# Weight scaling into PSUM, a PReLU that reads its product from PSUM, and a reordered first phase in a pooled-attention and feed-forward kernel

## The chip, the cores and the metric

The kernel runs on one core of a Trainium2 chip, so one set of engines works: TensorE (PE in the profile, with its weight loads PEld), VectorE (DVE), ScalarE (ACT), GpSimd (POOL) and SyncE (SP), which issues the DMAs. Each engine works through its own instruction list in order; semaphores make it wait for others. SBUF holds operands, PSUM takes matmul results and can be read and written by DVE and ACT. The metric is the device time of one execution in microseconds (us), and the median of several executions stands for a kernel. Beside these times there is one profiled execution with a trace of every instruction.

## The reference

Eight batches of eight heads, 576 positions and head size 64. Keys and values are first averaged over groups of 8 positions, so each query sees 72 keys. The attention output of all 4608 tokens, 512 wide, then goes through a two-layer network of inner size 2048 with a PReLU between.

```python
k_p = k.reshape(B, H, S // 8, 8, D).mean(axis=3)
v_p = v.reshape(B, H, S // 8, 8, D).mean(axis=3)
attn = softmax(q @ k_p.transpose(0, 1, 3, 2) / sqrt(D))
x = (attn @ v_p).transpose(0, 2, 1, 3).reshape(B * S, H * D)
h = x @ w_in
g = maximum(h, 0) + alpha * minimum(h, 0)
return g @ w_out
```

## The kernel before, in words

**Chunks.** The 4608 tokens are worked in nine chunks of 512. For a chunk the kernel makes scores, softmax and the mix with the pooled values (these give four transposed tiles x of 128x512), then the first layer in 16 steps f of 128 inner columns, then the second layer, which sums over the same 16 steps. Every matrix product is made of three fp16 products, because each operand is kept as a pair of fp16 numbers, high and low: low x high, high x low, high x high. A step of the first layer is 12 matmuls of 512 columns into one PSUM bank of the pool ps_h, which has two buffers ("h"). A step of the second layer is 12 matmuls too.

**PReLU.** For each step f, `ffn1_scaled` (ACT, L775) copies the bank h into an SBUF tile t times the per-row scale rp; that is the last reader of the bank, so the bank is free for step f+2 when it ends. `ffn1_prelu` (DVE, L779) then makes max(t x al, t) within SBUF. `ffn1_parts` makes the fp16 pair g: the high part on ACT (L786), the low part on POOL (L789).

**Weights.** The weights arrive as float64, read as pairs of 32-bit words. `load_w` brings two steps' weights in one DMA of 1024 KB into a "big" buffer (12 of them, shared with other inputs); `max_w` (DVE, L238) finds row maxima, from which power-of-two scales are made. `convert` makes fp16 pairs of them, eight tiles for each layer: ACT shifts the low word in place (L641); the high word, scaled, goes into an SBUF tile v (three buffers), by ACT in two halves for the first layer (L651) or by POOL in one piece for three of the eight tiles (L645, `v_pool=3`), by ACT in one piece for the second layer (L655); DVE then puts the words together with two bit operations over 128x1024 elements, L665 (shift v by 3, or the low word) and L669 (or the sign), both in SBUF. Then the fp16 high part is made by ACT (L688, L693) and the low part by POOL (L707 for the first layer; L702 for three of the 16 halves of the second, after one more ACT scaling, L700) or by DVE (L696, the other 13 halves).

**Order.** All of chunk 0, the conversion of the weights, and the attention of chunk 1 stand in one first phase, `start`. There a planner, the class `_Plan`, sets the order on all five engines: every operation has an assumed duration, a rank and the buffers it takes and gives, and at each point the planner emits the operation that could start first, by rank among those that could start almost at once. The ranks come from the table of numbers `RK`. Names of the buffers in the planner: "S" are the two buffers of the PSUM pool ps_s, which scores, pooled keys, maxima and the mix share; "h" the two banks; "v" the conversion tiles. Where PE would be idle for long, the planner puts in idle matmuls (L837). From chunk 1 on the order is not the planner's: a scheduler of the language sets it from the dependencies and its own durations, and the next chunk's attention is woven into the steps of the first layer. There the second layer of chunk c follows, and so on to chunk 8.

**Attention in the first phase.** A softmax of 128 tokens runs: row maxima on DVE (L507), subtraction (L521, for tiles that DVE serves), exp on ACT, sums (L526), L528 and L530 for the reciprocal, the product with it on POOL (L532), copies to fp16 pairs on ACT and POOL (L537, L540, L543), and a DMA that transposes. With four such tiles and the pooled values (L483) the mix (PE, L605) gives x, split into fp16 by ACT (L562) and DVE (L566), both reading PSUM.

Of the kernel before, what the change touches and what calls it, by code (L numbers as in the profile page):

```python
# [9 lines left out]
F32 = mybir.dt.float32  # L10
I32 = mybir.dt.int32
# [44 lines left out]
def _new_b(c):  # L56
# [16 lines left out]
class _Plan:  # L73
# [6 lines left out]

    HOP, DMA_HOP = 0.12, 2.0
# [3 lines left out]
    def __init__(self, fill, **room):  # L85
        self.fill = fill
        self.ops, self.room = [], {k: n * [0.0] for k, n in room.items()}

    def add(self, engine, us, emit, *after, rank=0.0, take=None, give=None):
        op = dict(engine=engine, us=us, emit=emit, after=after, rank=rank, n=len(self.ops),  # L90
                  take=take, give=(give,) if isinstance(give, str) else give or (), end=None)
        self.ops.append(op)
        return op

    def start(self, op, free):
# [3 lines left out]
        if op["take"]:  # L99
            t.append(min(self.room[op["take"]]))  # L100
        return max(t)

    def emit(self):
        free, left = {}, list(self.ops)
        while left:
# [14 lines left out]
            free[op["engine"]] = t + op["us"]  # L120
            op["end"] = t + op["us"] + (self.DMA_HOP if op["engine"] == "SP" else self.HOP)
# [9 lines left out]
def pooled_attention_prelu_ffn(ctx: ExitStack, tc: tile.TileContext, qT, kT, vT, kN, vN, w1, w2, alpha, out):  # L131
# [44 lines left out]
    eight = const.tile([P, 2], I32, name="eight")  # L176
    nc.vector.memset(eight, 8)
# [6 lines left out]
    m1 = const.tile([P, NF], F32, name="m1")  # L184
# [115 lines left out]
    def attention(add, c, bs, rank, begin=False, early=False, k_pool=0, q_cuts=1, on_act=(), on_dve=(), behind=()):  # L300
# [116 lines left out]
        for i, b in enumerate(bs):  # L417
            for j in range(2):
# [10 lines left out]
                kd.append(add("DVE", 0.6, lo, h, *kd[2 * i:], rank=rank, give="f" if j else None))  # L429
        qd = {}  # L430
        for i, (t, ld) in enumerate(ql):
# [4 lines left out]
            for a in range(0, HC, w):  # L436
# [8 lines left out]
                    h, *([qd[1]] if end else []), rank=rk,  # L445
# [8 lines left out]
        for b in bs:  # L454
# [21 lines left out]
            def vfloor(b=b, vr=vr):  # L476
# [8 lines left out]
                op0=ALU.mult, op1=ALU.subtract), x, rank=rank + rks["v"] + 1, give="f")  # L485
# [9 lines left out]
        for i in range(TPC):  # L495
# [24 lines left out]
            else:  # L520
# [12 lines left out]
                out=ex(), in0=ex(), in1=sm().broadcast_to([P, 2, 4, SP]), op=ALU.mult), x, rank=rk)  # L533
# [430 lines left out]
```

## Time and profile before

| | |
|---|---|
| time, median of 3 runs | 891.62 us (888.89 to 892.07) |
| the profiled execution's own time | 890.46 us |
| its span in the trace | 888.8 us |
| granted TensorE clock, mean of the span | 0.983 of full speed |
| PE busy | 847.1 us, 95% of the span |
| DVE, ACT, POOL busy | 452.9, 428.2, 400.5 us |
| mix of chunk 0 starts on PE | 63.2 us |
| first layer of chunk 0 done and second layer started | 118.5 us |
| first layer of chunk 1 starts | 177.3 us |

Times in the trace count from the span's start. A row of the trace's timeline gives start, duration, engine, line, operation, tiles and shapes (out <- in), and in brackets how long the engine had been idle before and what it then waited for. Rows that group instructions give the count, the total busy time, the mean in ns, and the idle time before them by what ended it. In the table of windows each engine's busy time stands for each stretch, with PEclk for the granted clock, 1.00 being full speed. The chain of waits is followed back from the last instruction, at each step to what released it.

### The profile page before, as it was taken

The page shows a single profiled execution, that of the slowest core. Times are in us where ns is not written, and L with a number is a line of the kernel's source. Part 1 is how long each engine was busy: PE and PEld are TensorE (multiplying, and loading weights), DVE is VectorE, ACT ScalarE, POOL GpSimd, SP SyncE. Part 2 cuts the span into 40 slices and gives each one's busy share as a digit, 9 for nine tenths or more (in the row PEclk, how much of TensorE's full clock was granted, in tenths as well). Part 3 has the DMA queues.
Part 4 walks back from the last instruction along what each step waited for, and adds up shares of the span by engine and source line. Part 5 has one row for each costly group of instructions (what it writes and reads, how often), then busy time and mean ns, then how long its engine had stood idle before and what let it go on. Part 6 is the DMA issues. An engine that isn't in the chain of part 4 may idle for free.

```text
span 888.8 us, 11503 instructions
## 1 busy us (share of the span) xinstructions
PE 847.1 (95%) x4447; PEld 411.1 (46%) x4447; DVE 452.9 (51%) x655; ACT 428.2 (48%) x724; POOL 400.5 (45%) x377
## 2 busy tenths in 40 slices
PE   6769997898999999999999999999999999999998
PEld 5444453344444544454445444544454444444443
DVE  4999999758415841583158315831583146112210
ACT  5967785555433643364336433643463346213330
POOL 1387948457714461456144614561456027202320
PEclk9879999999999999999999999999999999999999
DMA  9576312360621171117111611171115003100000
GB/s 339 198 158 268 124 51 51 75 202 9 157 96 40 25 182 56 39 28 192 43 39 28 178 57 38 29 198 37 39 28 119 36 13 70 26 36 12 1 25 24
DMA packets 93639, 74.75 MB, mean 84 GB/s; under 512 B 77040, under 2 KB 77616, under 8 KB 93584
## 3 DMA queue, kind: packets, MB, share of 16 engines
q1 hardware_dynamic: 93584, 74.01, 29.4%
q8 instruction: 35, 0.57, 0.3%
q14 instruction: 20, 0.16, 0.1%
HBM read 45.10 MB, written 9.44 MB: 61 GB/s over the span
## 4 chain that ended last, share of the span: by engine, by line
PE 81%; DVE 11%; POOL 3%; ACT 2%; DMA 2%; issue 2%; SPq 0%; POOLq 0%; ACTq 0%; DVEq 0%
PE o L815 13%; PE o L816 13%; PE o L817 13%; PE h L769 12%; PE h L770 12%; PE h L771 12%; PE x L605 2%; DVE v L665 2%; DVE t L779 2%; DVE m L238 1%; DMA vraw<-vT_dram 1%; PE s L595 1%; PE s L594 1%; PE s L596 1%; PE pl L283 1%
## 5 line engine op out<-in xcount | busy, mean ns | idle before, releaser
L789 POOL TENSOR_TENSOR g<-t,g 128x512 f16<-128x512 f32 x144 | 179.6, 1250 | 337.0 <-ACT g L786 337.0
L779 DVE SCALAR_TENSOR_TENSOR t<-t,al 128x512 f32<-128x512 f32 x144 | 140.5, 980 | 272.9 <-ACT t L775 266.1
L770 PE MATMUL h<-x,w 128*128 128x512 f16 x576 | 219.2, 381 | 2.4 <-DVE x L566 2.4
L769 PE MATMUL h<-x,w 128*128 128x512 f16 x576 | 219.1, 380 | 1.4 <-ACT o L805 1.4
L771 PE MATMUL h<-x,w 128*128 128x512 f16 x576 | 218.8, 380 | 0.0
L816 PE MATMUL o<-w,g 128*128 128x512 f16 x544 | 207.1, 381 | 4.4 <-POOL w L702 2.8
L815 PE MATMUL o<-w,g 128*128 128x512 f16 x544 | 206.7, 381 | 3.3 <-POOL g L789 2.8
L817 PE MATMUL o<-w,g 128*128 128x512 f16 x544 | 204.2, 381 | 0.0
L786 ACT CAST g<-t 128x512 f16<-128x512 f32 x144 | 88.4, 615 | 100.9 <-DVE t L779 100.5
L775 ACT ACTIVATE t<-h,rp 128x512 f32<-128x512 f32 x144 | 97.9, 681 | 67.1 <-PE h L771 63.7
L805 ACT ACTIVATE o<-o,os 128x512 f32<-128x512 f32 x34 | 23.2, 687 | 174.1 <-PE o L817 174.1
L815 PEld LDWEIGHTS <-g 128*128 128x128 f16 x576 | 56.5, 98 | 75.4 <-issue 6.0
L817 PEld LDWEIGHTS <-g 128*128 128x128 f16 x576 | 56.6, 98 | 73.8 <-issue 6.9
L771 PEld LDWEIGHTS <-w 128*128 128x128 f16 x576 | 56.5, 98 | 70.3 <-issue 3.5
L769 PEld LDWEIGHTS <-w 128*128 128x128 f16 x576 | 56.5, 98 | 68.1 <-issue 3.7
L816 PEld LDWEIGHTS <-g 128*128 128x128 f16 x576 | 56.5, 98 | 67.4 <-issue 2.1
L770 PEld LDWEIGHTS <-w 128*128 128x128 f16 x576 | 56.5, 98 | 65.4 <-issue 2.5
L463 POOL TENSOR_TENSOR vraw<-vraw 72x512 f32<-72x512 f32 (+1 forms) x56 | 58.9, 1069 | 56.7 <-DMA vraw<-vT_dram 45.8
L566 DVE SCALAR_TENSOR_TENSOR x<-x,xsc,x 128x512 f16<-128x512 f32 x36 | 25.8, 747 | 69.7 <-ACT x L562 69.7
L532 POOL TENSOR_TENSOR e<-e,sm 128x576 f32<-128x576 f32 x35 | 46.9, 1341 | 25.5 <-DVE sm L530 17.2
L537 ACT CAST apad<-e 128x576 f16<-128x576 f32 x72 | 44.8, 669 | 25.8 <-POOL e L532 18.0
L540 POOL TENSOR_TENSOR apad<-e,apad 128x448 f16<-128x448 f32 x36 | 41.7, 1158 | 3.3 <-ACT apad L537 3.1
(135 smaller groups left out, 886.0 us busy)
## 6 DMA issues: line engine op xcount, KB each, us to landing
w<-w_dram SPq DMA_DIRECT2D x16, 1024.0 KB
out_dram<-o SPq DMA_DIRECT2D x36, 256.0 KB
qraw<-qT_dram SPq DMA_DIRECT2D x17, 512.0 KB
vraw<-vT_dram SPq DMA_DIRECT2D x28, 288.0 KB
kraw<-kT_dram SPq DMA_DIRECT2D x12, 576.0 KB
kq<-kT_dram SPq DMA_DIRECT2D x2, 576.0 KB
nat<-kN_dram SPq DMA_DIRECT2D x2, 512.0 KB
nat<-vN_dram SPq DMA_DIRECT2D x2, 512.0 KB
```

The lines of the kernel that those rows point to most:

```text
L463: nc.gpsimd.tensor_tensor(out=o, in0=y, in1=z, op=ALU.add)
L532: x = add("DVE" if i in on_dve else "Pool", us, lambda ex=ex, sm=sm, eng=eng: eng.tensor_tensor(out=ex(), in0=ex(), in1=sm().broadcast_to( ...
L769: nc.tensor.matmul(ps, w[:, 1, ks_], x[:, 0], start=(n == 0), stop=False)
L770: nc.tensor.matmul(ps, w[:, 0, ks_], x[:, 1], start=False, stop=False)
L771: nc.tensor.matmul(ps, w[:, 0, ks_], x[:, 0], start=False, stop=(n == NK - 1))
L775: nc.scalar.activation(t, hps.pop((c, f)), AF.Copy, scale=rp[:, f:f + 1])
L779: nc.vector.scalar_tensor_tensor(out=t, in0=t, scalar=al[:, f:f + 1], in1=t, op0=ALU.mult, op1=ALU.max)
L786: nc.scalar.copy(out=g[:, 0], in_=t)
L789: nc.gpsimd.tensor_tensor(out=g[:, 1], in0=t, in1=g[:, 0], op=ALU.subtract)
L815: nc.tensor.matmul(ps, g[:, 1, ts_], w[:, 0], start=(f == 0), stop=False)
L816: nc.tensor.matmul(ps, g[:, 0, ts_], w[:, 1], start=False, stop=False)
L817: nc.tensor.matmul(ps, g[:, 0, ts_], w[:, 0], start=False, stop=(f == NF - 1))
```

## The change

Six edits:

1. In 14 of the 16 weight tiles (`ps1=6` of the first layer's eight, `ps2=8` of the second's) the first scaling of the high word is written to PSUM, to a buffer of the pool ps_s ("S"), in place of SBUF. Both bit operations of DVE then have one operand in PSUM (L660, L663, formerly L665, L669); the second writes its result to the SBUF tile v, and only then is the S buffer given back.
2. `ffn1_prelu` (now L776) takes its first operand from the bank h in PSUM and multiplies by ra = rp x al instead of al; t is the second operand as before. So DVE's PReLU, not ACT's scaling, is the last reader of the bank, in all nine chunks. ra costs one small POOL product for each of four groups (L725).
3. No tile's first scaling is on POOL any more: the three POOL operations (L645) become six halves on ACT (L653). The unused variant with the shift on POOL is gone, with its constant `eight`.
4. All 16 low halves of the second layer's weights are made on DVE (`w2_dve=16`): three POOL products (L702) and three ACT scalings (L700) become three DVE operations (L691, formerly L696).
5. The small product `ds` (L585, formerly L581) is a tensor_scalar in place of a scalar_tensor_tensor.
6. The planner has a rule for a shared port: POOL operations, and DVE operations marked `two=`, are not planned to overlap. Bit operations with a PSUM operand and the PReLU are not marked. Durations and all ranks in `RK` are new, which gives a new order for the first phase.

```diff
-RK = dict(k_pool=1, sh1_pool=0, sh2_pool=0, v_pool=3, s_pool=0, w2_dve=13, lo_dve=0, l1=392.23, step=2.57,
+RK = dict(k_pool=1, ps1=6, ps2=8, s_pool=0, w2_dve=16, lo_dve=0, l1=405.5, step=2.27, l2=548.61, mx1=198.3,
...
+        if op["two"]:
+            t.append(self.port)
         return max(t)
...
+            if op["two"]:
+                self.port = t + op["us"]
...
-    m1 = const.tile([P, NF], F32, name="m1")
+    m1 = ra = const.tile([P, NF], F32, name="m1")
...
-                nc.vector.scalar_tensor_tensor(out=ds[a:z], in0=eq[c, i // 2][a:z], scalar=2.0 ** -32,
-                                               in1=ek[b][a:z], op0=ALU.mult, op1=ALU.mult)
+                nc.vector.tensor_scalar(out=ds[a:z], in0=eq[c, i // 2][a:z], scalar1=2.0 ** -32,
+                                        scalar2=ek[b][a:z], op0=ALU.mult, op1=ALU.mult)
...
+        ps = once(lambda: ps_s.tile([P, 2, CH], F32, tag="s", name="vw"))
+        by_ps = wide and picked(i, RK[f"ps{l}"], NF // 2)
+        u, kind = (ps, "S") if by_ps else (v, "v")
...
-        if l == 1 and picked(i, RK["v_pool"], NF // 2):
-            x = add("Pool", 2.4, lambda: nc.gpsimd.tensor_tensor(
-                out=v(), in0=word(l, i, 1), in1=y1[:, 2 * i:2 * i + 2].broadcast_to([P, 2, 512]), op=ALU.mult),
-                begin, rank=rank, take="v")
-        elif l == 1:
+        if l == 1:
             x = begin
             for j in range(2):
-                x = add("ACT", 0.61, lambda j=j: nc.scalar.activation(
-                    v()[:, j], word(l, i, 1)[:, j], AF.Copy, scale=y1[:, 2 * i + j:2 * i + j + 1]),
-                    begin, x, rank=rank, take=None if j else "v")
+                x = add("ACT", 0.66, lambda j=j: nc.scalar.activation(
+                    u()[:, j], word(l, i, 1)[:, j], AF.Copy, scale=y1[:, 2 * i + j:2 * i + j + 1]),
+                    begin, x, rank=rank, take=None if j else kind)
...
         if wide:
-            x = add("DVE", 1.5, lambda: nc.vector.scalar_tensor_tensor(
-                out=vi(), in0=word(l, i, 1).bitcast(I32), scalar=-2 ** 31, in1=vi(),
-                op0=ALU.bitwise_and, op1=ALU.bitwise_or), x, rank=rank, give="big" if i % 2 else None)
+            x = add("DVE", 1.22, lambda: nc.vector.scalar_tensor_tensor(
+                out=u().bitcast(I32), in0=u().bitcast(I32), scalar=3, in1=word(l, i, 0).bitcast(I32),
+                op0=ALU.logical_shift_left, op1=ALU.bitwise_or), x, low, rank=rank, two=not by_ps)
+            x = add("DVE", 1.22, lambda: nc.vector.scalar_tensor_tensor(
+                out=v().bitcast(I32), in0=word(l, i, 1).bitcast(I32), scalar=-2 ** 31, in1=u().bitcast(I32),
+                op0=ALU.bitwise_and, op1=ALU.bitwise_or), x, rank=rank, two=not by_ps,
+                take="v" if by_ps else None, give=(*(["big"] if i % 2 else []), *(["S"] if by_ps else [])))
...
-        nc.scalar.activation(t, hps.pop((c, f)), AF.Copy, scale=rp[:, f:f + 1])
+        nc.scalar.activation(t, hps[c, f], AF.Copy, scale=rp[:, f:f + 1])
...
-        nc.vector.scalar_tensor_tensor(out=t, in0=t, scalar=al[:, f:f + 1], in1=t, op0=ALU.mult, op1=ALU.max)
+        nc.vector.scalar_tensor_tensor(out=t, in0=hps.pop((c, f)), scalar=ra[:, f:f + 1], in1=t,
+                                       op0=ALU.mult, op1=ALU.max)
```

The first place where the order differs and that matters below is on DVE in the softmax of the fourth token tile of chunk 0, from the subtraction of the maxima to the reciprocal. "pt" and "pr" belong to reductions of maxima over partitions, "e_123" (after: "e_121"), "rp" and "y" to scales of the first layer's weights, "ev" and "vs__" to the scale of the pooled values. Before:

```order
L521 TENSOR_TENSOR e<-s,mx 128x576
L208 TENSOR_REDUCE pt<-pm 128x1
L213 TENSOR_SCALAR pr<-pt 128x1
L226 TENSOR_SCALAR e_123<-pr 128x4
L229 TENSOR_SCALAR ev_528<-pr 128x1
L718 TENSOR_SCALAR rp<-e_123 128x4
L234 TENSOR_SCALAR vs__532<-ev_528 128x1
L526 TENSOR_REDUCE sm<-e 128x8
L718 TENSOR_SCALAR y_127<-rp 128x4
L528 TENSOR_SCALAR sm<-sm 128x8
L718 TENSOR_SCALAR rp<-rp 128x4
L530 RECIPROCAL sm<-sm 128x8
```

The same place with the change:

```order
L525 TENSOR_TENSOR e<-s,mx 128x576
L242 TENSOR_REDUCE vm<-vs 72x1
L530 TENSOR_REDUCE sm<-e 128x8
L212 TENSOR_REDUCE pt<-pm 128x1
L217 TENSOR_SCALAR pr<-pt 128x1
L532 TENSOR_SCALAR sm<-sm 128x8
L233 TENSOR_SCALAR ev_518<-pr 128x1
L534 RECIPROCAL sm<-sm 128x8
```

The three small operations on the weights' scale (L718, now L713) have moved behind the reciprocal, and the sum of the softmax stands closer to its subtraction.

The second place is on DVE from the last split of x to the second step of the first layer of chunk 0. "x" is the attention's output, "m_125" (after: "m_123") are maxima of the second layer's weights, "w_" loaded weights, "vw" a weight tile in PSUM. Before:

```order
L665 SCALAR_TENSOR_TENSOR v<-v,w_272 128x1024
L566 SCALAR_TENSOR_TENSOR x_676<-x,xsc,x_676 128x512
...
L566 SCALAR_TENSOR_TENSOR x_688<-x,xsc,x_688 128x512
L238 TENSOR_REDUCE m_125<-w_664 128x2
L669 SCALAR_TENSOR_TENSOR v<-w_272,v 128x1024
L779 SCALAR_TENSOR_TENSOR t<-t,al 128x512
L238 TENSOR_REDUCE m_125<-w_686 128x2
L238 TENSOR_REDUCE m_125<-w_707 128x2
L779 SCALAR_TENSOR_TENSOR t<-t,al 128x512 x2
```

With the change:

```order
L663 SCALAR_TENSOR_TENSOR v<-w_217,vw 128x1024
L570 SCALAR_TENSOR_TENSOR x_663<-x,xsc,x_663 128x512
L570 SCALAR_TENSOR_TENSOR x_666<-x,xsc,x_666 128x512
L242 TENSOR_REDUCE m_123<-w_605 128x2
L570 SCALAR_TENSOR_TENSOR x_687<-x,xsc,x_687 128x512
L570 SCALAR_TENSOR_TENSOR x_693<-x,xsc,x_693 128x512
L713 TENSOR_SCALAR rp<-rp 128x6
L660 SCALAR_TENSOR_TENSOR v<-v,w_241 128x1024
L660 SCALAR_TENSOR_TENSOR vw<-vw,w_270 128x1024
L776 SCALAR_TENSOR_TENSOR t<-h,m_122,t 128x512
L663 SCALAR_TENSOR_TENSOR v<-w_241,v 128x1024
L663 SCALAR_TENSOR_TENSOR v<-w_270,vw 128x1024
```

Ahead of the first split of x stand 11 bit operations of the first layer's weights before, and eight with the change; the other eight now stand among the PReLUs.

The third place is on PE where the first layer of chunk 0 ends and the second begins: "g" are the outputs of the PReLU, "s" scores of chunk 1, "idle" matmuls without use. Before, 38 idle matmuls stand there (a weight load and a matmul each) and the 60 score matmuls of chunk 1 come later, behind the seventh step of the second layer and after:

```order
L771 MATMUL h<-x_688,w_282 128x512
L837 LDWEIGHTS pool
L837 MATMUL idle<-pool 128x256
...
L815 LDWEIGHTS g
L815 MATMUL o<-w_664,g 128x512
```

With the change 36 score matmuls of chunk 1 stand there:

```order
L768 MATMUL h<-x_693,w_280 128x512
L598 LDWEIGHTS q_982
L598 MATMUL s<-kbd_95,q_982 128x144
...
L600 MATMUL s<-kbd_95,q_982 64x144
L813 LDWEIGHTS g
L813 MATMUL o<-w_605,g 128x512
```

The remaining 24 of the 60 score matmuls come after the third and the fourth step of the second layer.

More of the change, by code (lines that the diff above doesn't have):

```diff
@@ L86, in __init__, with add @@
         self.fill = fill
-        self.ops, self.room = [], {k: n * [0.0] for k, n in room.items()}
-    def add(self, engine, us, emit, *after, rank=0.0, take=None, give=None):
+        self.ops, self.room, self.port = [], {k: n * [0.0] for k, n in room.items()}, 0.0
+    def add(self, engine, us, emit, *after, rank=0.0, take=None, give=None, two=False):
         op = dict(engine=engine, us=us, emit=emit, after=after, rank=rank, n=len(self.ops),
-                  take=take, give=(give,) if isinstance(give, str) else give or (), end=None)
+                  take=take, give=(give,) if isinstance(give, str) else give or (), end=None,
+                  two=two or engine == "Pool")
         self.ops.append(op)
@@ L428, in attention @@
                 h = add("ACT", 0.53, hi, scs[0], rank=rank)
-                kd.append(add("DVE", 0.6, lo, h, *kd[2 * i:], rank=rank, give="f" if j else None))
+                kd.append(add("DVE", 0.6, lo, h, *kd[2 * i:], rank=rank, give="f" if j else None, two=True))
         qd = {}
@@ L444, in attention @@
                     op0=ALU.mult, op1=ALU.subtract),
-                    h, *([qd[1]] if end else []), rank=rk,
+                    h, *([qd[1]] if end else []), rank=rk, two=True,
                         give="big" if end else "aT" if early and a + w == HC else None)
@@ L638, in convert @@
         v = once(lambda: wp.tile([P, 2, 512], F32, tag="v", name="v", bufs=ROOM["v"]))
-        by_pool = wide and picked(i, RK[f"sh{l}_pool"], NF // 2)
-        if wide and not by_pool:
-            low = add("ACT", 1.2, lambda: nc.scalar.activation(
+        ps = once(lambda: ps_s.tile([P, 2, CH], F32, tag="s", name="vw"))
+        by_ps = wide and picked(i, RK[f"ps{l}"], NF // 2)
+        u, kind = (ps, "S") if by_ps else (v, "v")
+        if wide:
+            low = add("ACT", 1.15, lambda: nc.scalar.activation(
@@ L706, in convert @@
         dve = l == 1 and picked(i, RK["lo_dve"], NF // 2)
-        x = add("DVE" if dve else "Pool", 1.5 if dve else 2.4, lambda: (nc.vector if dve else nc.gpsimd).tensor_tensor(
-            out=part(1), in0=v(), in1=part(0), op=ALU.subtract), x, rank=rank + RK[f"lo{l}"], give="v")
+        x = add("DVE" if dve else "Pool", 1.25 if dve else 2.3, lambda: (nc.vector if dve else nc.gpsimd).tensor_tensor(
+            out=part(1), in0=v(), in1=part(0), op=ALU.subtract), x, rank=rank + RK[f"lo{l}"], give="v", two=dve)
         return [x, x]
@@ L718, in small @@
             return add("DVE", 0.2, lambda: nc.vector.tensor_scalar(
-                out=out, in0=in0, scalar1=s1, scalar2=s2_, op0=op0, op1=op1), x, rank=rank)
+                out=out, in0=in0, scalar1=s1, scalar2=s2_, op0=op0, op1=op1), x, rank=rank, two=True)
         x = add("DVE", 0.2, lambda: floor2(r[0], e1[:, fs], wide), x, rank=rank)
```

43 lines of the change are left out of this document (16 added, 27 removed).

## The prediction, made before the changed kernel ran

> **What bounds the kernel now.** I read the table of windows first, cut where one stage of the kernel hands over to the next: attention of chunk 0 (to 67), first layer of chunk 0 (to 118.5), second layer of chunk 0 (to 170.7), then the chunks after it.
>
> ```profile
> core 0: us, PE busy (x) PEld busy (x) DVE busy (x) ACT busy (x) POOL busy (x), PEclk, DMA share, GB/s
> 0.00:67.06 67.06, 44.68 (x251) 30.49 (x252) 52.73 (x99) 48.14 (x102) 32.35 (x35) 0.87 0.74 233
> 67.06:118.52 51.46, 47.38 (x231) 22.85 (x231) 49.36 (x51) 39.37 (x56) 42.34 (x25) 0.97 0.42 167
> 118.52:170.67 52.15, 45.41 (x244) 21.60 (x244) 49.10 (x61) 34.40 (x74) 34.19 (x32) 0.93 0.33 75
> ...
> 260.00:800.00 540.00, 540.00 (x2867) 257.84 (x2866) 244.07 (x360) 235.91 (x380) 226.97 (x226) 1.00 0.25 65
> ```
>
> From 260 to 800 PE is busy for 540.00 of 540.00 us at full clock: nothing can be gained there, only lost. In the second and third rows DVE is busy for 49 of 51 to 52 us, which is the bound of the first phase (PE's 47.38 there holds idle matmuls too). The chain of waits says the same where the first layer of chunk 0 ends:
>
> ```profile
> 102.63 1.22 DVE m L238
> ...
> 112.79 1.99 DVE v L665
> 114.78 0.16 DVE s L752
> ...
> 114.96 0.73 ACT w L693
> ...
> 116.51 1.97 POOL w L702
> 118.52 0.38 PE o L816
> ...
> 119.33 0.22 PE o L816
> ```
>
> The second layer's first matmul hangs on DVE's row of maxima and bit operations, then on ACT and POOL. In the last row PE goes on at 0.216 us a matmul (0.22 in the chain), so that a step of 12 matmuls takes 2.59 us when nothing stops it.
>
> Third, what DVE does in the first 171 us, in groups by form (busy us and mean ns of one stand behind the bar):
>
> ```profile
> L665 DVE SCALAR_TENSOR_TENSOR v<-v,w 128x1024 int32<-128x1024 int32 x16 | 25.4, 1589 | 0.0
> L669 DVE SCALAR_TENSOR_TENSOR v<-w,v 128x1024 int32<-128x1024 int32 x16 | 21.8, 1364 | 0.0
> L779 DVE SCALAR_TENSOR_TENSOR t<-t,al 128x512 f32<-128x512 f32 x16 | 17.7, 1129 | 0.4 <-ACT t L775 0.4
> L696 DVE SCALAR_TENSOR_TENSOR w<-v,s,w 128x512 f16<-128x512 f32 x13 | 15.1, 1174 | 0.9 <-ACT w L693 0.8
> L581 DVE SCALAR_TENSOR_TENSOR ds<-e 128x1 f32<-128x1 f32 x4 | 4.6, 1151 | 0.0
> L645 POOL TENSOR_TENSOR v<-w,y 128x1024 f32<-128x1024 f32 x3 | 7.0, 2329 | 11.1 <-DVE y L718 9.7 <-issue 1.4
> L702 POOL TENSOR_TENSOR w<-v,w 128x512 f16<-128x512 f32 x3 | 4.4, 1460 | 6.7 <-ACT v L700 6.7
> L651 ACT ACTIVATE v<-w,y 128x512 f32<-128x512 f32 x10 | 7.1, 752 | 0.0
> ```
>
> These means are longer than the same operations need alone, as the timeline shows:
>
> ```profile
> 48.47 2.12 POOL L707 TENSOR_TENSOR w<-v,w 128x1024 f16<-128x1024 f32 x1
> 48.50 0.15 DVE L229 TENSOR_SCALAR ev<-pr 128x1 int32<-128x1 int32 x1
> 48.58 2.04 DVE L718 TENSOR_SCALAR rp<-e 128x4 int32<-128x4 int32 x1
> ...
> 57.52 1.22 DVE L665 SCALAR_TENSOR_TENSOR v<-v,w 128x1024 int32<-128x1024 int32 x1
> ...
> 114.85 0.74 DVE L779 SCALAR_TENSOR_TENSOR t<-t,al 128x512 f32<-128x512 f32 x1
> ```
>
> L718 works on four elements a row and takes 2.04 us, until POOL's L707 is done at 50.59; the 128x1 operation beside it takes 0.15. So some DVE operations with SBUF operands wait out a running POOL operation. Against 1.22 and 0.74 us alone, the groups lose 16 x 0.37 = 5.9 us (L665), 16 x 0.14 = 2.3 (L669), 16 x 0.39 = 6.2 (L779), 13 x 0.43 = 5.6 (L696, of L779's shape) and 4 x 1.0 = 4.0 (L581, against 0.15): 24 us together. An operation of the same kind with a PSUM operand, in the whole run:
>
> ```profile
> L566 DVE SCALAR_TENSOR_TENSOR x<-x,xsc,x 128x512 f16<-128x512 f32 x36 | 25.8, 747 | 69.7 <-ACT x L562 69.7
> ```
>
> Its mean over 36 is 0.747, the time alone: it never waited. The change makes 28 of the 32 bit operations and all PReLUs of this kind.
>
> **The change, stage by stage.** *To the mix of chunk 0.* The softmax of the fourth token tile is last before the mix:
>
> ```profile
> 45.80 0.74 DVE L507 TENSOR_REDUCE mx<-s 128x8 f32<-128x576 f32 x1
> ...
> 52.02 0.20 DVE L530 RECIPROCAL sm<-sm 128x8 f32<-128x8 f32 x1
> ...
> 63.23 1.93 PE L605 MATMUL x<-aT,v 88*64 88x512 f16 x16 [1.37 <-DVE v L665]
> ...
> 67.86 0.58 PE L770 MATMUL h<-x,w 128*128 128x512 f16 x1 [2.38 <-DVE x L566]
> ```
>
> From maxima to reciprocal are 6.4 us. With the three L718 and their 128x4 maxima behind it, there remain maxima, subtraction, another reduction and the sum at 0.74 each and five small ones at 0.15: 3.7, so -2.7 us. Ahead of the split of x, DVE has eight bit operations for 11: 3 x 1.22 = -3.7, of which 2.38 is the wait of L770 on L566. Together -6.4 us. Against it, ACT gets the six halves for L645: 6 x 0.752 = 4.5 us; ACT was busy for 48.14 of 67.06, so idle time covers most, and I charge 0.9. This stage: -5.5; bounds -2 (only the wait of L770 goes) and -8 (the port waits of L645 go as well, 3 x 0.5).
>
> *First layer of chunk 0.* DVE now has 16 PReLUs (11.8 us at 0.74), 16 bit operations (19.5 at 1.22), 8 maxima (9.8 by L238's 1.22), 4 splits (3.0) and 4 of L691 (3.0), which is 47.1; key sums and products and small ones I put at 6, an estimate from rows between 0.15 and 1.4 us; 48 of these start 0.07 before the one ahead ends, -3.4. That is 49.7, plus 1 to 2 us of port waits on what remains in SBUF: 51 against 51.46, so -0.5, bounds -4 and +3. DVE stays the bound here and is still what frees the h banks, now by the PReLU, behind which bit operations stand: a late PReLU delays the matmuls of step f+2. But the stage now does more: 16 bit operations of the 32 where nine or ten were, and at its end 36 scores in place of idle matmuls (36 x 144/512 x 0.216 = 2.2 us).
>
> *Second layer of chunk 0.* PE lost time in three waits:
>
> ```profile
> 143.23 0.38 PE L816 MATMUL o<-w,g 128*128 128x512 f16 x1 [1.41 <-DVE w L696]
> ...
> 153.35 0.26 PE L205 MATMUL pm<-pd,ones 128*128 128x128 bf16 x1 [3.23 <-ACT pd L202]
> ...
> 156.19 0.58 PE L816 MATMUL o<-w,g 128*128 128x512 f16 x1 [1.65 <-POOL w L702]
> ```
>
> After the last, matmuls take 0.58 in place of 0.38 for a while (the stage's clock is 0.93), about 1.5 us more. DVE has 49.1 us here before. Seven bit operations go ahead (7 x 1.48 = 10.3 at the means), one L696 on balance (1.2), and ds loses its 4.0: 33.6. Then PE sets the stage: 15 steps x 2.59 = 38.9, 24 scores 1.5, and I leave 3.2 for waits that remain: 43.6 against 52.15, so -8.5; bounds -11 (no wait) and -4 (half). L702 and L700 become DVE's L691: 3 x 0.74 on an engine that now has room, nothing. Should DVE be late here, the next step waits, at up to 1.22 for each bit operation ahead.
>
> *The chunks after.* The h bank now comes free when the PReLU ends, not when ACT's scaling ends, on an engine that is 100% busy. Put against the trace of before, the PReLU of step f ends after the start of step f+2 in 20 steps of the chunks 1 to 7, by 13.1 us in sum. First, worst and last of them:
>
> ```profile
> 185.05 0.74 DVE L779 SCALAR_TENSOR_TENSOR t<-t,al 128x512 f32<-128x512 f32 x1
> 185.05 0.38 PE L769 MATMUL h<-x,w 128*128 128x512 f16 x1
> ...
> 293.66 0.38 PE L769 MATMUL h<-x,w 128*128 128x512 f16 x1
> 294.48 0.73 DVE L779 SCALAR_TENSOR_TENSOR t<-t,al 128x512 f32<-128x512 f32 x1
> ...
> 677.06 0.78 DVE L779 SCALAR_TENSOR_TENSOR t<-t,al 128x512 f32<-128x512 f32 x1 [4.71 <-ACT t L775]
> 677.52 0.38 PE L769 MATMUL h<-x,w 128*128 128x512 f16 x1
> ```
>
> They are late by 0.74, 1.55 and 0.32. After one stall PE is behind, and the next PReLU is less late or not at all, so the largest of each chunk is the better guess: 6.0 in sum. And the order around two of these places (chunk 2) has 0.5 to 1.2 us more of other matmuls ahead of the step, and PReLUs no longer wait for POOL (mean 1.13 to 0.74). I take +2.5, bounds 0 and 13.1. The new small POOL products of ra, four of 128x2 to 128x6, stand far ahead of the first PReLU and cost nothing.
>
> *The sum:* -5.5 - 0.5 - 8.5 + 2.5 = -12.0 on the profiled execution's 890.46, so 878.5. The median of the runs shown is 1.2 above it: **879.6 us** forecast.
>
> **The rivals.**
> *A: the hold of the h bank costs every chunk.* As forecast, but +6 to +13: 883 to 890, at its middle 885. For it: 20 late steps. Against it: another order. 0.14.
> *B: the first phase only changes its bound.* The two S buffers now carry weight tiles from ACT's scaling to DVE's second bit operation, beside scores, maxima and mix; a score that waits for a bit operation and a bit operation that waits for a softmax would be the new chain. This also holds the case that a PSUM operand does not spare the wait, against which L566 speaks. Half of 14.5 remains: 891.6 - 7.2 + 2.5 = 887, 885 to 890. 0.16.
> *C: slower.* One mechanism: the PReLU's hold stops PE in the chunks after, all 20 latenesses count (13.1), and the six places late by more than 1 us lower the granted clock, at 1.5 us each as after 156.19: 13.1 + 9 = 22 against a gain of 14.5, so 891.6 + 7.5 = 899. It decides once such a pause lowers the clock; the pause of 1.41 before 143.23 left it whole (0.38 after it), the two near 153 to 156 did not. 0.09.
> *D: the second layer and the attention reach their bounds,* -11 and -8, with -4 between: 891.6 - 23 = 868.6. 0.07.
> *E: a PSUM operand is dearer by itself.* From rows, L566 at 0.747 against L779 alone at 0.74 makes it 0.007 us, or 0.2 us over the 32 bit operations and PReLUs of the stage that DVE bounds: nothing. 0.04 that it is as much as a tenth of L566, 0.075 each: 32 x 0.075 = +2.4, 882.0. The Trainium skill, "Perfetto Trace Analysis", section "Optimizing Scalar/DVE Operations", speaks for this rival: it gives a fixed DVE overhead of about 60 ns with SBUF and 125 ns with PSUM operands, so by that page 32 x 0.065 = 2.1 us (an estimate); no row here shows such a difference.
>
> **How the numbers follow.** Forecast 0.50 (871 to 886), A 0.14, B 0.16, C 0.09, D 0.07, E 0.04. A difference under 0.5%, 4.5 us, cannot be told from none here, so the border is 887.2. Faster: 0.50 + D 0.07 + E 0.04 + 0.10 of A + 0.05 of B = 0.76. Same: the rest of A and B, 0.15. Slower: C, 0.09. The range from 868 to 891 takes in D, A and B and leaves C and some tails out.
>
> **What would show it.** Bit operations with a PSUM operand at 1.22 and L776 at 0.74 on average, beside running POOL operations. The mix at about 58 to 60 in place of 63.2, the first layer's 16 steps still DVE-bound in about 51 us, the second layer of chunk 0 in 43 to 45 us with DVE well under PE. In the chunks after, rows of L766 that wait for L776: none or few short ones for the forecast, one or more of over 1 us in each chunk for A, and a clock under 1.00 after them for C. For B, matmuls L598 or scalings L653 and L657 that wait for an S buffer. The forecast is wrong if the first layer of chunk 1 does not start by about 166 (177.3 before), or if PE is not busy throughout from there on.

## The result, and the profile after

The changed kernel takes 902.8 us (median of 4 runs, 899.47 to 903.77) against 891.15 us before (median of 4 runs, 888.89 to 892.07): a ratio of 1.0128, 95% interval 1.0095 to 1.0161. It is slower by 1.3%, a small loss but clear of the spread of the runs. The forecast was 879.6 us with a range up to 891.

The loss is not where most of the change was made. The table of windows, first of before, then of the changed kernel, is cut at four events: first matmul of chunk 0's first layer, first matmul of its second layer, first matmul of chunk 1's first layer, end.

```profile
0.00:65.09 65.09, 44.29 (x250) 30.38 (x251) 50.76 (x98) 46.17 (x99) 30.38 (x34) 0.87 0.73 227
65.09:116.95 51.86, 47.39 (x233) 22.86 (x232) 49.91 (x51) 39.77 (x57) 42.74 (x25) 0.97 0.46 180
116.95:177.28 60.33, 50.65 (x290) 24.22 (x288) 53.69 (x70) 39.12 (x82) 35.76 (x33) 0.94 0.29 65
177.28:888.80 711.52, 704.75 (x3678) 333.64 (x3677) 298.58 (x438) 303.18 (x489) 291.60 (x287) 1.00 0.25 66
```

```profile
0.00:62.03 62.03, 40.88 (x246) 28.42 (x246) 42.94 (x95) 47.27 (x101) 20.24 (x34) 0.91 0.80 257
62.03:115.15 53.12, 48.16 (x234) 21.71 (x233) 50.39 (x70) 49.54 (x74) 31.35 (x26) 0.94 0.42 165
115.15:161.71 46.56, 45.18 (x252) 21.33 (x250) 34.96 (x57) 28.86 (x66) 23.94 (x30) 1.00 0.36 72
161.71:901.70 739.99, 712.63 (x3678) 334.35 (x3677) 278.95 (x438) 304.93 (x489) 272.23 (x287) 0.99 0.24 63
```

Up to chunk 1 the change gains 177.28 - 161.71 = 15.6 us, nearly all in the second layer of chunk 0 (60.3 to 46.6 us, DVE no longer near its bound). The eight chunks after it lose 740.0 - 711.5 = 28.5 us with the same 3678 matmuls, in another order. PE there stands idle for 739.99 - 712.63 = 27.4 us in place of 6.8, and is busy for 7.9 us more with the same instructions, at a clock of 0.99.

What PE waits for in that last stage stands in the groups of instructions, again before and after (in rows of L776, m is the tile of ra):

```profile
L769 PE MATMUL h<-x,w 128*128 128x512 f16 x512 | 194.3, 380 | 1.4 <-ACT o L805 1.4
L815 PE MATMUL o<-w,g 128*128 128x512 f16 x512 | 194.1, 380 | 2.9 <-POOL g L789 2.8 <-ACT o L805 0.2
```

```profile
L766 PE MATMUL h<-x,w 128*128 128x512 f16 x512 | 194.3, 382 | 14.3 <-DVE t L776 12.9 <-ACT o L803 1.4
L813 PE MATMUL o<-w,g 128*128 128x512 f16 x512 | 194.0, 380 | 10.7 <-POOL g L787 10.5 <-ACT o L803 0.2
```

Two kinds of wait, of about the same size: the first layer waits 12.9 us for the PReLU, which frees the h bank, and the second layer waits 10.5 us for POOL's low half of g. Before, there was none of the first and 2.8 us of the second. The 12.9 us are seven waits: one of 1.6 to 2.6 us in each of the chunks 1 to 6, and one of 0.43 in chunk 2.

One wait of the first kind, in the timeline of chunk 2 of the changed kernel:

```profile
271.47 1.48 DVE L217 TENSOR_SCALAR pr<-pt 128x3 f32<-128x3 f32 x1
272.87 0.74 DVE L776 SCALAR_TENSOR_TENSOR t<-h,m,t 128x512 f32<-128x512 f32 x1
273.46 1.15 POOL L787 TENSOR_TENSOR g<-t,g 128x512 f16<-128x512 f32 x1
273.53 2.79 DVE L233 TENSOR_SCALAR e<-pr 128x3 int32<-128x3 int32 x1
...
274.57 0.61 POOL L467 TENSOR_TENSOR vraw<-vraw 72x256 f32<-72x256 f32 x1
275.14 1.15 POOL L787 TENSOR_TENSOR g<-t,g 128x512 f16<-128x512 f32 x1
...
277.30 1.36 DVE L429 SCALAR_TENSOR_TENSOR kbd<-ks,s,kbd 64x288 f16<-64x288 f32 x2
277.85 2.19 ACT L442 ACTIVATE q<-qraw,s 128x1024 f16<-128x1024 f32 x2
279.03 2.48 DVE L446 SCALAR_TENSOR_TENSOR q<-qraw,s,q 128x1024 f16<-128x1024 f32 x2 [0.37 <-ACT q L442]
279.94 1.24 ACT L772 ACTIVATE t<-h,rp 128x512 f32<-128x512 f32 x2
281.43 0.75 DVE L776 SCALAR_TENSOR_TENSOR t<-h,m,t 128x512 f32<-128x512 f32 x1
...
282.23 0.38 PE L766 MATMUL h<-x,w 128*128 128x512 f16 x1 [2.32 <-DVE t L776]
```

A 128x3 operation (L233) takes 2.79 us: it ends when the third of three POOL operations ends that follow each other without a gap. All of the key and query work on DVE and ACT follows it, and the PReLU stands behind that. (Before, the same operation took 1.08 us in each of these chunks, behind one POOL operation.) ACT's scaling of this bank is the first of the two L772, done at about 280.6; the PReLU ends at 282.18, and PE starts at 282.23. With the release by ACT, PE would have gone on some 1.6 us earlier. After this pause the trace has seven matmuls some 0.42 us apart in place of 0.216; after the pause of 3.43 us, shown next, it has nine.

One wait of the second kind, at the end of chunk 1's first layer:

```profile
226.99 0.75 DVE L776 SCALAR_TENSOR_TENSOR t<-h,m,t 128x512 f32<-128x512 f32 x1 [5.14 <-ACT t L772]
...
227.78 0.62 ACT L784 CAST g<-t 128x512 f16<-128x512 f32 x1 [0.89 <-DVE t L776]
...
230.76 3.06 POOL L467 TENSOR_TENSOR vraw<-vraw 72x512 f32<-72x512 f32 x3 [7.03 <-DMA vraw<-vT_dram]
233.78 1.15 POOL L787 TENSOR_TENSOR g<-t,g 128x512 f16<-128x512 f32 x1
...
234.99 0.39 PE L813 MATMUL o<-w,g 128*128 128x512 f16 x1 [3.43 <-POOL g L787]
```

The high half of g is ready at 228.40. POOL stands idle, because the next chunk's value additions (L467) come first in its queue and their DMA lands only at 230.7. PE, which keeps to its own list, has nothing ahead of the matmul that waits: in the new order the second layer's matmuls stand in pieces between the steps of the first layer, the last two of 18 and 15, and 14 are left behind the last step to cover the latency of g, where the order of before keeps 45 (237.7 to 247.4 in its trace). At the ends of the first layer in the chunks 1 to 7 the new order has 10 to 26 matmuls there before the mix, the old one 45 to 50. Nobody wrote this order: the language's scheduler made it, and e1 below shows that it follows from the PReLU's operand alone. Not all of the 10.5 us are of this kind. Four waits, 8.4 us, stand behind additions that waited for a DMA; one of 1.20 stands behind additions that did not, and one of 0.92 is in chunk 8, which has no additions.

### The profile page after: what moved, and what is told of

Its sections match the earlier page's. It is cut to its first block, busy times and chain, and to the rows that moved or that the text cites. A ratio compares the mean times of both kernels' runs of the same rounds, so it can differ in the third digit from the quotient of the medians.

```text
span 901.7 us, 11443 instructions
## 1 busy us (share of the span) xinstructions
PE 846.9 (94%) x4404; PEld 405.8 (45%) x4404; DVE 407.2 (45%) x657; ACT 430.6 (48%) x727; POOL 347.8 (39%) x375
## 4 chain that ended last, share of the span: by engine, by line
PE 65%; DVE 11%; issue 7%; ACT 6%; DMA 6%; POOL 4%; SPq 1%; POOLq 0%; DVEq 0%; ACTq 0%
PE o L813 10%; PE o L814 10%; PE o L815 10%; PE h L766 9%; PE h L767 9%; PE h L768 9%; DMA vraw<-vT_dram 3%; POOL g L787 3%; DVE t L776 2%; DVE e L233 2%; DVE q L446 1%; PE x L609 1%; DMA nat<-kN_dram 1%; SPq L254 1%; ACT q L442 1%
## 5 line engine op out<-in xcount | busy, mean ns | idle before, releaser
L787 POOL TENSOR_TENSOR g<-t,g 128x512 f16<-128x512 f32 x144 | 166.9, 1160 | 397.7 <-ACT g L784 393.4
L776 DVE SCALAR_TENSOR_TENSOR t<-h,m,t 128x512 f32<-128x512 f32 x144 | 107.0, 744 | 308.4 <-ACT t L772 303.7
L813 PE MATMUL o<-w,g 128*128 128x512 f16 x544 | 206.1, 380 | 10.7 <-POOL g L787 10.5
L772 ACT ACTIVATE t<-h,rp 128x512 f32<-128x512 f32 x144 | 97.5, 682 | 117.4 <-PE h L768 96.2
L803 ACT ACTIVATE o<-o,os 128x512 f32<-128x512 f32 x34 | 23.1, 687 | 156.3 <-PE o L815 156.3
L813 PEld LDWEIGHTS <-g 128*128 128x128 f16 x576 | 56.3, 98 | 79.7 <-POOL g L787 13.1
L467 POOL TENSOR_TENSOR vraw<-vraw 72x512 f32<-72x512 f32 (+1 forms) x56 | 53.7, 972 | 43.0 <-DMA vraw<-vT_dram 39.2
L536 POOL TENSOR_TENSOR e<-e,sm 128x576 f32<-128x576 f32 x35 | 40.5, 1158 | 34.6 <-DVE sm L534 33.6
L544 POOL TENSOR_TENSOR apad<-e,apad 128x448 f16<-128x448 f32 x36 | 37.3, 1035 | 17.7 <-ACT apad L541 17.6
```

What stands on the lines that cost most here:

```text
L467: nc.gpsimd.tensor_tensor(out=o, in0=y, in1=z, op=ALU.add)
L772: nc.scalar.activation(t, hps[c, f], AF.Copy, scale=rp[:, f:f + 1])
L776: nc.vector.scalar_tensor_tensor(out=t, in0=hps.pop((c, f)), scalar=ra[:, f:f + 1], in1=t, op0=ALU.mult, op1=ALU.max)
L787: nc.gpsimd.tensor_tensor(out=g[:, 1], in0=t, in1=g[:, 0], op=ALU.subtract)
L813: nc.tensor.matmul(ps, g[:, 1, ts_], w[:, 0], start=(f == 0), stop=False)
```

## The experiments

Theory H: all of the loss comes from the PReLU being the last reader of the bank in the chunks after the first phase, through the wait itself and through the order that the scheduler makes around it. Rival S: it comes from something else that the change leaves behind there.

### e1 and e2: the hold taken away, and the hold alone

e1 keeps everything but the PReLU of the chunks 1 to 8:

```diff
-        nc.vector.scalar_tensor_tensor(out=t, in0=hps.pop((c, f)), scalar=ra[:, f:f + 1], in1=t,
-                                       op0=ALU.mult, op1=ALU.max)
+        u, by = (hps.pop((c, f)), ra) if c == 0 else (t, al)
+        nc.vector.scalar_tensor_tensor(out=t, in0=u, scalar=by[:, f:f + 1], in1=t, op0=ALU.mult, op1=ALU.max)
```

> The changed kernel, with the PReLU reading the bank in PSUM in chunk 0 only; in chunks 1 to 8 ACT's scaling is again the last reader of the bank and the PReLU works within SBUF. Theory H (the hold of the h bank by the PReLU, and the order that the scheduler makes around it, costs the chunks after the first phase): all of the 28.5 us lost after the first step of chunk 1 (740.0 us in the changed kernel against 711.5 before) comes back, the first phase keeps its 15.6 us: 872 to 878 us, no row of the first layer's first matmul that waits for the PReLU for more than 0.5 us. Rival S (the loss comes from something else that the change leaves behind in the chunks after, such as the order at the end of the first phase or where loads of later chunks start): 895 to 903.

Measured: 874.04 us, ratio 0.9824 (0.9796 to 0.9852) to before. Its last stage in the table of windows, and the two groups of waits:

```profile
162.23:871.70 709.47, 703.21 (x3678) 333.27 (x3677) 298.40 (x438) 303.14 (x489) 294.03 (x287) 1.00 0.25 66
```

```profile
L766 PE MATMUL h<-x,w 128*128 128x512 f16 x512 | 194.1, 379 | 1.6 <-ACT o L803 1.4 <-ACT t L772 0.2
L813 PE MATMUL o<-w,g 128*128 128x512 f16 x512 | 193.6, 379 | 1.8 <-POOL g L787 1.6 <-ACT o L803 0.2
```

The waits for the PReLU are gone and those for POOL are down to 1.6 us, from 2.8 before the change. The stage takes 709.5 us, a little less than before the change. Its matmuls on PE stand in the same order as before the change, one for one. The first phase keeps its gain.

e2 is the opposite: the kernel before, with its own order of the first phase, and only the PReLU changed (the bank as first operand, ra as its factor, in all chunks).

> The kernel before, with the PReLU alone changed to read its product from PSUM in all nine chunks; the planner's order of the first phase as before. Theory H: the chunks after lose 25 to 32 us as in the changed kernel, so the first layer of chunk 1 starts at 174 to 180 and the whole takes 913 to 922 us. Rival S: 886 to 894.

Measured: 922.35 us in a single run. The groups of its last stage:

```profile
L771 PE MATMUL h<-x,w 128*128 128x512 f16 x512 | 195.1, 383 | 13.4 <-DVE t L781 12.0 <-ACT o L808 1.4
L818 PE MATMUL o<-w,g 128*128 128x512 f16 x512 | 193.7, 379 | 11.8 <-POOL g L792 11.6 <-ACT o L808 0.2
```

The same two waits, 12.0 and 11.6 us; the stage takes 741.8 us against 711.5, so +30.3, and the order on PE in it is that of the changed kernel, one for one. Theory H holds in both directions, S falls. Also, the first phase did not gain by the PSUM operand of the PReLU here: the first layer of chunk 1 starts at 178.8 against 177.3, although the 16 PReLUs went from 1.13 to 0.75 us each. The waits for the bank do not explain that: the last matmul of chunk 0's first layer comes at 112.49 against 112.59, and the loss appears behind it, where the second layer starts at 119.74 against 116.95. Its cause was not followed.

### e5, e6 and e7: the two waits, one at a time

All three keep the PReLU on PSUM in all chunks. e5 takes the port wait of the three small 128x3 operations away by doing one column at a time, with the same order on PE:

```diff
-                floor2(r[0], e()[:, cols])
+                for j in each:
+                    floor2(r[0][:, j] if c > 1 else r[0], e()[:, j])
...
-            scs.append(add("DVE", 0.2, lambda cols=cols: recip(s()[:, cols], e()[:, cols], 13), x, rank=rk))
+            scs.append(add("DVE", 0.2, lambda each=each: [recip(s()[:, j], e()[:, j], 13) for j in each], x, rank=rk))
```

> The changed kernel, with the three small DVE operations that make the scales of queries and keys (L217, L233, L238, 128x3 each) done one column at a time (128x1) for the attention of chunks 2 to 8; the order on PE is the same. In the changed kernel L233 takes 2.79 us at 273.5 because POOL runs, and all that follows on DVE (ds, kbd, the split of q) stands ahead of the PReLU that frees the h bank. Theory P (the bank is late because this port wait pushes DVE's row back): the waits of the first layer for the PReLU fall from 12.9 us after 161.7 to under 4, and the time by 9 to 14 us to 888 to 894. Rival Q (the split of q itself, 2.48 us on DVE behind ACT's, makes the PReLU late): waits stay above 9 us, 897 to 903.

Measured: 889.18 us, single run. Timeline at the same place, and the groups of the last stage:

```profile
271.46 1.84 POOL L471 TENSOR_TENSOR vraw<-vraw 72x512 f32<-72x512 f32 x2
272.03 0.27 DVE L235 TENSOR_SCALAR e<-pr 128x1 int32<-128x1 int32 x3
272.14 0.62 ACT L788 CAST g<-t 128x512 f16<-128x512 f32 x1 [0.87 <-DVE t L780]
272.21 0.27 DVE L240 TENSOR_SCALAR s<-e 128x1 int32<-128x1 int32 x3
```

```profile
L817 PE MATMUL o<-w,g 128*128 128x512 f16 x512 | 194.2, 380 | 12.4 <-POOL g L791 12.2 <-ACT o L807 0.2
L770 PE MATMUL h<-x,w 128*128 128x512 f16 x512 | 193.0, 379 | 2.6 <-ACT o L807 1.4 <-DVE t L780 1.1
```

Three operations of 128x1 take 0.27 us while POOL runs, where one of 128x3 took 2.79. The waits for the PReLU fall from 12.9 to 1.1 us, the time by 13.6. The order on PE is the same in both, one for one. So the split of q that stands just ahead of the PReLU (rival Q) is not what made it late: it was early enough once the port wait ahead of it was gone. Which of the three small operations counts most, e5 does not separate. POOL's waits stay.

e6 leaves the small operations as they are and places the next chunk's value work behind the 16 steps of the first layer:

```diff
-            attention(line.add, c + 1, _new_b(c + 1), 0.0)
+            attention(line.add, c + 1, _new_b(c + 1), 0.0, vadd=late.add)
...
+            late.emit(len(late.ops))
         for i in range(TPC):
             ffn2(c, i)
```

> The changed kernel, with the pooling of the next chunk's values (POOL's additions L467, which wait for a DMA, and what follows them) placed behind the 16 steps of the first layer, so that they no longer stand ahead of a low half of g on POOL. If the second kind of wait (second layer waits for POOL's g, 10.5 us after 161.7) comes from these additions standing ahead in the queue, it falls under 3 us, the waits on the PReLU stay, and the time falls by 8 to 13 us to 889 to 895. If the distance on PE between the last step of the first layer and its products is too short by itself, waits of 1 us and more on g stay: 897 to 903.

Measured: 881.94 us, single run:

```profile
L767 PE MATMUL h<-x,w 128*128 128x512 f16 x512 | 193.7, 379 | 5.5 <-DVE t L777 4.2 <-ACT o L804 1.4
L814 PE MATMUL o<-w,g 128*128 128x512 f16 x512 | 193.2, 379 | 2.1 <-POOL vm L476 0.9 <-POOL g L788 0.9 <-ACT o L804 0.2
```

POOL's waits fall from 10.5 to 1.8 us, as expected. The edit also made a new order on PE, so this is not the additions alone; but at the ends of the chunks 3 and 5, where both orders have 22 matmuls between the last step of the first layer and the mix, waits of 1.15 and 1.39 us are gone too. The time fell by more than expected (20.9 us), since the waits for the PReLU fell too, to 4.2. Not because the port was free: L233's counterpart still takes 2.79 us in five chunks. What differs is the order on PE; how it spares these waits was not followed further. So this kernel does not take one kind of wait away alone; e5 does.

> Both edits of e5 and e6 in one, the PReLU reading PSUM in all chunks. If these two are all that the hold of the bank does, the time comes to 874 to 881 us, as with the hold taken away (874.0). If the scheduler's order around the hold costs beside them, 884 to 896.

With both edits: 878.71 us, single run, waits for the PReLU 0.4 us and for POOL 4.3. That is within the 874 to 881 expected. The order on PE is that of e6. With the small operations by column and the value work moved, the kernel comes to within 5 us of e1, although the PReLU still holds the bank; of POOL's 4.3 us, 2.5 are one wait behind additions in chunk 1. How much of the rest of the gain is due to e6's new order was not separated.

### e3, e4, e9 and e10: what the first phase gains by

e4 is the changed kernel with the old PReLU in all chunks, order of the first phase unchanged:

> The changed kernel with the PReLU within SBUF in all nine chunks, the planner's order of the first phase unchanged. Against e1 this shows what the PSUM operand of the 16 PReLUs of chunk 0 is worth: the 16 lose about 0.39 us each beside POOL again (1.13 against 0.74), of which some stands on the path, while the bank comes free earlier; I expect the first layer of chunk 1 at 162 to 166 and 0 to 4 us more than e1, and the chunks after as in e1 (711 to 713 us).

Measured: 874.3 us, single run. The 16 PReLUs of chunk 0 take 1.00 us each in place of 0.75, and the first layer of chunk 1 starts at 163.65 against 162.23 in e1: 1.4 us, as expected. That is more than the 0.5 us by which the changed kernel and e1, whose first phase is the same, differ at this point, but each is one trace. In the whole time it makes no difference that a single run could tell. So edit 2 gains 1 to 2 us in the first phase, in this order, and loses 28 after it.

e3 scales all weight tiles into SBUF:

```diff
-RK = dict(k_pool=1, ps1=6, ps2=8, s_pool=0, w2_dve=16, lo_dve=0, l1=405.5, step=2.27, l2=548.61, mx1=198.3,
+RK = dict(k_pool=1, ps1=0, ps2=0, s_pool=0, w2_dve=16, lo_dve=0, l1=405.5, step=2.27, l2=548.61, mx1=198.3,
```

> As e1, but all weight tiles are scaled into SBUF (none into PSUM), in the order that the planner then makes with its port rule and the same ranks. If the PSUM operand of the bit operations is what shortened the first phase, the bit operations take 1.4 to 1.6 us on average again or stand behind POOL, and the first layer of chunk 1 starts at 170 to 178 in place of 161.7: 882 to 890 us. If the new order and the port rule did it, it starts at 161 to 165: 872 to 879 us.

Measured: 907.31 us, outside both expectations. It does not answer the question. With other buffers taken, the planner makes another order from the same ranks, and a bad one: the first layer of chunk 0 takes 85.3 us, with 173 idle matmuls in one place. It shows only that the ranks fit one set of durations and buffers.

e9 asks the same with the order held: the planner still plans all fourteen tiles as before this edit, but ten of them are worked in SBUF.

```diff
-        u, kind = (ps, "S") if by_ps else (v, "v")
+        u, kind = (ps if l == 2 and i < 4 else v, "S") if by_ps else (v, "v")
```

> As e1 (874.0 us, first layer of chunk 1 at 162.2), with the first scaling of ten of the fourteen tiles (all six of the first layer, the last four of the second) put into the SBUF tile v again and the bit operations done in place; the order on DVE and PE stays that of e1. If the PSUM operand is what the first phase gains by: the 20 bit operations go from 1.22 to 1.5 us on average, 5 to 6 us more on DVE, of which most stands on the path, and the first layer of chunk 1 starts 4 to 8 us later: 878 to 882 us. If the order is what it gains by: 0 to 2 us, 874 to 876.

Measured: 882.03 us, ratio 0.9913 (0.9882 to 0.9944) to before. The groups of DVE's bit operations, and of L691, up to 169 us:

```profile
L663 DVE SCALAR_TENSOR_TENSOR v<-w,v 128x1024 int32<-128x1024 int32 x12 | 18.3, 1531 | 0.0
L660 DVE SCALAR_TENSOR_TENSOR v<-v,w 128x1024 int32<-128x1024 int32 x12 | 17.4, 1461 | 0.0
L691 DVE SCALAR_TENSOR_TENSOR w<-v,s,w 128x512 f16<-128x512 f32 x16 | 17.4, 1120 | 0.1
...
L660 DVE SCALAR_TENSOR_TENSOR vw<-vw,w 128x1024 int32<-128x1024 int32 x4 | 4.9, 1222 | 0.0
L663 DVE SCALAR_TENSOR_TENSOR v<-w,vw 128x1024 int32<-128x1024 int32 x4 | 4.9, 1215 | 0.0
```

Side by side in one kernel: bit operations in SBUF 1.46 and 1.53 us on average, with a PSUM operand 1.22. 24 x 0.28 = 6.6 us more on DVE, and the first layer of chunk 1 starts at 169.07 against 162.23, 6.8 us later. That the two nearly agree does not show that just this stands on the path: L691, which the edit does not touch, takes 1.12 us in place of the 0.88 of e1, 3.9 us more, and DVE is busy for 12.8 us more in all up to that point. So the words in PSUM (edit 1) are worth 7 of the 15.6 us, with ten of fourteen tiles, in an order that was planned for operands in PSUM, and with what their longer operations do to others. Not separated are the other four tiles, the removal of L645 from POOL and the order itself; the rest of the 15.6 us lies with these and the PReLU's 1.4.

e10 gives `ds` its old two-tensor form in e1:

> As e1, with ds made by the two-tensor form of before (L581 then), same order. Before, the four of the first phase took 1.15 us each beside POOL, against 0.15 alone. In e1 they stand where the planner keeps most POOL work away from DVE or not: I expect 0.5 to 1.15 us each, 2 to 4 us more on DVE, of which half stands on the path: the first layer of chunk 1 0 to 2 us later, 874 to 876 us; in the chunks after nothing.

Measured: 875.31 us, single run; the first layer of chunk 1 at 161.64 against 162.23. The four take 0.38 us on average against 0.20 in e1 and 1.15 before. POOL runs beside one of the four only: that one takes 1.10 us beside L536, where the tensor_scalar of e1 at the same place takes 0.21; the other three take 0.14 to 0.15. The expected 2 to 4 us on DVE were 0.7, and in this order the edit shows no effect on the time.

### e8 and e11: a faster version

In e1 the first matmul of chunk 1 waits 1.38 us for ACT's L803, which empties an h bank that held a sum of the second layer. e8 sums in another order in the last step:

```diff
-            for i in range(TPC):
+            for i in (2, 3, 0, 1) if f == NF - 1 else range(TPC):
                 ffn2_step(0, i, f, acc[i])
```

> As e1 (PReLU from PSUM in chunk 0 only, 874.0 us), with one more edit: in the last step of chunk 0's second layer the four token tiles are summed in the order 2, 3, 0, 1, so that the two sums which stand in h banks end six matmuls (1.3 us) earlier and ACT empties them earlier. The wait of the first matmul of chunk 1 (1.37 us on ACT's L803, at 160.5 in e1) falls to under 0.3 us and the time by 1 to 2 us: 872 to 873.5. If the next wait (on POOL's g, 1.37 us at 186 in e1) grows by as much, nothing: 874.

Measured: 873.21 us, ratio 0.9813 (0.9786 to 0.9840); the wait stayed at 1.38 us. The time lies in the expected range, but the wait that was to give it did not move. The expectation named the wrong releaser: ACT's L803 stood idle for 1.76 us until DVE's small product os (L797), which is queued behind the splits of x. e11 makes these products at the ninth step:

```diff
+            if f == 8:
+                [out_scale(0, i) for i in range(TPC)]
```

> As e8 (873.2 us; its wait of 1.38 us before the first matmul of chunk 1 stayed, since ACT's L803 waited for the small DVE product os, L797, behind the splits of x), with these products made at the ninth step of chunk 0's second layer. The wait before the first matmul of chunk 1 falls under 0.3 us: 871.5 to 872.5 us, unless the next wait, near 186, takes it up.

Measured: 871.35 us (870.81 to 871.50), ratio 0.9787 (0.9762 to 0.9812). The timeline at the start of chunk 1:

```profile
159.09 1.28 ACT L803 ACTIVATE o<-h,os 128x512 f32<-128x512 f32 x2
160.18 0.38 PE L766 MATMUL h<-x,w 128*128 128x512 f16 x1
```

The wait is gone (no idle time stands in brackets), and chunk 1 starts at 160.18. This version is faster than before by 2.1% and than the changed kernel by 3.5% (medians of different runs). Its interval overlaps that of e1, so what e8 and e11 add to e1 is shown by the wait in the trace, and hardly by the times.

## Why the prediction was right or wrong

- **The first phase: right in sum, in part by luck.** Forecast -5.5 - 0.5 - 8.5 = -14.5 us, measured -15.6. Its parts miss by 2.4, 1.8 and 5.3 us, and the misses partly cancel: the mix starts at 58.2, as forecast, 5.0 us earlier, but only 3.1 of it is left at the first matmul of the first layer; the first layer of chunk 0 takes 1.3 us more, not 0.5 less; and its second layer 13.8 less (60.3 to 46.6, on events a little later than the forecast's windows).
- **The PSUM operand does not wait for POOL: right.** The 28 bit operations with it took 1.22 to 1.23 us on average and none over 1.26, 22 of them beside a running POOL operation. The 144 PReLUs took 0.74 and none over 0.78, 56 of them beside one.
- **Rival E fell.** With a PSUM operand L660 takes 1.228 us (14 operations), within SBUF 1.216 (the two that remain there): 0.01 us. The Trainium skill, "Perfetto Trace Analysis", section "Optimizing Scalar/DVE Operations", gives a DVE overhead of about 60 ns on SBUF and 125 ns on PSUM, 65 ns between the two. No such difference shows in these 0.01 us.
- **The chunks after: wrong, and this decided the time.** The step that failed is the term of +2.5 us, with 0 and 13.1 as bounds; it measured +28.5. The prediction's own sign of being wrong was met here: the first layer of chunk 1 started by 166, at 161.7, but PE was not busy throughout from there on. The term had three faults. First, its size: it took one stall a chunk, 6.0 us in sum, and then less than half of that. One stall a chunk is what came, in the chunks 1 to 6, but the stalls summed to 12.9 us, because L217, L233 and L238 ahead of the PReLU waited for POOL (e5: 1.1 us without that). The latenesses of before could not show this, since they came from an order that the change replaced; that all 20 of them sum to 13.1 is luck. The reasons for going below 6.0 were assumed, not priced. Second, the waits for POOL's g (10.5 against 2.8 us) were not seen at all: a longer hold of a buffer changes not only the wait but the order that a scheduler makes, and the cover at the end of the first layer went with it. Third, the upper bound held no clock: busy time on PE grew by 7.9 us, in which three slow stretches after pauses account for 4.8, against 1.7 in one before, so 3.1 more. The other 4.8 of the 7.9 us were not followed.
- **Rival C came nearest, at 0.09, but not by its own sum.** It said 899 us: all 20 latenesses (13.1) and a lower clock after six pauses (9), on a gain of 14.5. Measured: seven waits with 12.9 in sum, 3.1 more by the clock after three pauses (two of them waits for the PReLU), 4.8 more busy time besides, 7.7 more waits for POOL, which it did not have, and a gain of 15.6, together +12.9 from 890.46 to 903.40 in the profiled executions. That it comes so near is in part luck. Its chance was too low because the prediction took an engine that is 100% busy as one on which lateness is mostly absorbed; with the order on PE held, taking 11.8 us of such waits away gave 13.6 us (e5).
- **Rival A** had the mechanism, and a price of 6 to 13 us without clock or POOL. **Rival B** (the S buffers as new chain) and **D** did not occur: the first phase's sum stayed near the forecast, between half of it and D's -23.
- **The port in the chunks after** stood in the quoted rows (L718 at 2.04 us on four elements a row) and was not carried to the place where it counted: the same kind of small operation stands ahead of the PReLU, the longest (L233) at 2.79 us in five of the eight chunks, and e5 shows that the three of them are what made the PReLU late.

## What to carry to other kernels

Before the last reader of a double buffer is moved to another engine, look at what is queued ahead of the new reader on its engine, in the steady state and not only where the change is aimed at. Where the producer is fully busy, do not count on such lateness being absorbed, and do not price it from the old trace alone: where a scheduler sets the order, a new hold can make a new order, with other waits ahead of the new reader. Compare the orders around the ends of loops for work that used to cover a latency. A gain in one stage and a loss in another are best had apart: here the form of the PReLU chosen by chunk turned 1.3% slower into 1.8% faster.

## What the runs showed of the hardware

- A tensor_scalar of 128x3 took up to 2.79 us beside POOL, three of 128x1 together 0.27. The two-tensor form took 1.10 us with 128x1 beside a POOL operation where the tensor_scalar took 0.21 (e10, e1). So the wait depends on the form and the shape. How long it lasts depends on more: the 2.79 us span three POOL operations that follow each other without a gap, but in the kernel before, the same operation ended with the first:

```profile
286.24 1.15 POOL L789 TENSOR_TENSOR g<-t,g 128x512 f16<-128x512 f32 x1
286.34 1.08 DVE L229 TENSOR_SCALAR e<-pr 128x3 int32<-128x3 int32 x1
287.35 0.78 POOL L463 TENSOR_TENSOR vs<-vraw 72x128 f32<-72x128 f32 x2
```

  Here too POOL goes on without a gap, and DVE is let in. What decides is open.
- The granted clock after a pause of PE depends on more than the pause's length. In the changed kernel pauses of 2.48, 2.72 and 3.59 us (start to start, less one matmul) were followed by 7 to 9 matmuls at half speed, which cost 1.4 to 1.7 us a pause; others of 2.45 and 2.46 us were followed by one slow matmul or none. The traces show what else counts. In each trace all records of the granted clock begin on one grid of 3.413 us. The table of windows, cut on this grid around the pause of 2.48 us (in 279.97 to 283.38) and that of 2.46 us (ending at 656.13, across a line of the grid):

```profile
279.97:283.38 3.41, 1.15 (x6) 0.55 (x6) 3.41 (x5) 2.21 (x5) 0.48 (x1) 1.00 0.00 0
283.38:286.80 3.42, 3.42 (x14) 1.52 (x13) 0.28 (x2) 0.91 (x2) 1.87 (x3) 0.50 0.00 0
652.02:655.43 3.41, 1.82 (x9) 0.71 (x8) 3.01 (x4) 3.07 (x4) 0.00 (x0) 1.00 0.00 0
655.43:658.84 3.41, 2.71 (x15) 1.29 (x15) 1.89 (x3) 1.61 (x3) 1.95 (x2) 1.00 0.00 0
```

  The first pause leaves PE idle for 2.26 us of one window, and the next window has a clock of 0.50. The second is split, 1.60 and 0.70 us, and the clock stays at 1.00. In the 13 traces of this case, from 60 us on, all 24 windows with 1.98 us or more of idle time were followed by half clock, and of some 3070 with less, one (1.85 us, in the mix of the kernel before).
